# Taking a pair of heads through each pass of 256 rows in one group of four tiles, also where the pass crosses two batches

## The chip, the cores and the metric

The kernel runs on one core of a Trainium2 chip. The metric is the device time of one execution in microseconds; the changed kernel is compared with the kernel before on the same chip.

## What is computed

`q`, `k` and `v` have 8 batches, 8 heads, 576 rows and 64 columns a head. Attention keeps the 32 largest scores of each row; the result, reshaped to rows of 512, goes through a channel mix whose input is blended with the row before it.

```
scores = scale * np.matmul(q, k.transpose(0, 1, 3, 2))
kth = np.partition(scores, -top_k, axis=-1)[..., -top_k:-top_k + 1]
scores = np.where(scores >= kth, scores, -1000000000.0)
attn = np.exp(scores - np.max(scores, axis=-1, keepdims=True))
attn = attn / (np.sum(attn, axis=-1, keepdims=True) + 1e-09)
x = np.matmul(attn, v)                      # then (B, S, 512)
xk = mu_k * x + (1.0 - mu_k) * x_prev       # x_prev: the row before, 0 at a batch's start
xr = mu_r * x + (1.0 - mu_r) * x_prev
k = np.maximum(xk @ w_k, 0.0)
out = 1.0 / (1.0 + np.exp(-(xr @ w_r))) * (k * k @ w_v)
```

## The kernel before

**Tiles and slots.** A tile is 128 partitions of scores against all 576 keys. Mostly these are 128 rows of one head; two heads (a pair, `hp`, 0 to 3) and 128 rows make two tiles. A unit of four tiles is a pair of heads and 256 rows, a unit of two is 128 rows, and a unit of one tile is 64 rows of both heads. There are 288 tiles, and the program is written out by hand as a software pipeline of one slot a tile: `ORDER` lists the steps of a slot, and in slot n tile n is scored (`scores`, `keep`), tile n−1 and n−2 go through the search for the largest (`candidates`, `best`, `drop`), n−3 is counted (`count` on ACT, `below` on POOL: the tile `sg`), n−4 masked, n−5 turned (`turn_tile`), and behind the last tile of a unit (n−6) its sums are turned (`turn_inverse`) and its values weighed (`weigh`, PE), then taken out (`take_sums`, ACT) and multiplied into `xT` (`place`, POOL).

**Passes.** I call 16 slots, that is 256 of the 4608 rows for all four pairs, a pass, and number them 0 to 17. A batch ends inside passes 2, 4, 6, 11, 13 and 15. `PARTS` says how the 576 rows of each batch are cut, and a pass with an end of a batch is taken in two rounds: the rest of the old batch for all four pairs, then the start of the next for all four. In passes 2, 6, 11 and 15 the cut falls at 64 or 192 rows, so units of one tile occur.

**Loads.** Keys of a pair have one of four homes (`KEYS`); SP issues all loads and stores in the program's order, keys and queries four or five slots ahead, values (two buffers) when the unit two before has been weighed.

**Channel mix.** For each 256 finished rows a chunk starts (`chunks`, `have`, `begin`): POOL blends (`xd`, `xm`), ACT and POOL split into `xh` and `xl`, and PE multiplies in steps of three matmuls (`three`): 8 into `pz`, 32 into `ph`, and, for the chunk before, 16 into `pv`. Between `ph` and `pv` stand ACT (`r`, `hh`) and POOL (`r`, `hl`), in units of two blocks of 128; the last `pv` of a tile of rows needs the last `hl`. Two or one of these steps make a piece, and `work` deals pieces into the slots by a budget of PE time: `L.use("pe", ...)` books the steps of attention, and a piece goes in while enough is left. POOL and ACT work of the mix is dealt in the same way (`L.soft`). From slot 252 on (`END`, `HASTE`) the budget is looser. Each chunk so follows some two passes behind, and behind the last score what is left is drained, with DVE in place of POOL (`g.by`).

**Spared rows.** A chunk that starts in one batch and ends in the next first copies the rest of the old batch into `rest` (`save`), so that its buffer comes free.

Of the kernel before, what the change touches and what calls it, by code (L numbers as in the profile page):

```python
# [47 lines left out]
def topk_attention_channel_mix(ctx: ExitStack, tc: tile.TileContext, q, k, v, mu_k, mu_r, w_k, w_v, w_r, out):  # L48
# [31 lines left out]
    def open_pools(stack, g, sfx):  # L80
# [102 lines left out]
    def load_v(g, P, batch, hp):
        P.v = g.two.tile([128, 2, NKC, D], F32, name="v_in")
        P.vr = vr_hf[P.n % 2]
        h = heads(v, batch, hp)
        for j in range(2):
            nc.sync.dma_start(P.v[:, j], h[j, :MAIN].rearrange("(c p) d -> p c d", p=128))
        nc.sync.dma_start(P.vr[64:], h[:, MAIN:].rearrange("h p d -> p h d"))

    def units_of(shape):

        units, tiles = [], []
        for row, w in shape:
            U = Env()
            U.row, U.w = row, w
            units.append(U)
            for k in range(w):
                T = Env()
                T.U, T.k, T.t, T.u, T.j, T.row = U, k, len(tiles), k // 2, k % 2, row + k // 2 * 128  # L200
                T.last = k == w - 1
                tiles.append(T)
        return units, tiles
# [85 lines left out]
    def inverse(g, U):  # L289
        rs = U.rs[:, :U.w]  # L290
        nc.scalar.activation(rs, rs, AF.Copy, bias=1e-9)

    def inverse2(U):
        rs = U.rs[:, :U.w]
        nc.vector.reciprocal(rs, rs)

    def spread(g, U):
        w, d = U.w, 64 if U.w > 1 else 128
        U.rb = g.one.tile([128, w, d], F32, name="rb")
        nc.gpsimd.tensor_scalar(U.rb, U.rs[:, :w, None].to_broadcast([128, w, d]), 1.0, 1.0, op0=OP.mult, op1=OP.mult)  # L300

    def turn_inverse(g, U, L):
        rb = U.rb.rearrange("p h d -> p (h d)")
        pr = g.pt[:, :, 384:]
        n = (U.w + 1) // 2
        for u in range(n):
            nc.tensor.transpose(pr[:, u], rb[:, u * 128:(u + 1) * 128], ident)

        def out_():
            U.ri = g.two.tile([128, 256], F32, name="ri")  # L310
            if U.w > 1:
                nc.scalar.activation(U.ri[:, :n * 128].rearrange("p (u q) -> p u q", u=n), pr[:, :n], AF.Copy)
            else:
                for j in range(2):
                    h = slice(j * 64, (j + 1) * 64)
                    nc.scalar.activation(U.ri[h, :64], pr[h, 0, h], AF.Copy)
        L.at(0, "late", out_)

    def weigh(g, U, u):
        P = U.P  # L320
        if u == 0:
            U.pa = g.sums[U.w == 1]
        hs = [slice(j * 64, (j + 1) * 64) for j in range(2)]
        if U.w > 1:
            pa = U.pa[:, u]
            ms = [[U.et[u, j][:, c, :] for j in range(2)] for c in range(NKC + 1)]
        else:
            pa = U.pa
            ms = [[U.et[0, 0][:, c, h] for h in hs] for c in range(NKC + 1)]
        for c in range(NKC + 1):  # L330
            for j in range(2):
# [288 lines left out]
    def pipeline(g):  # L620
# [360 lines left out]
```

## Time and profile before

| | us |
|---|---|
| median of 3 runs (1161.68 to 1163.26) | 1162.88 |
| the profiled execution | 1162.55 |
| its span | 1160.7 |
| busy: PE, DVE, ACT, POOL | 1094.9, 1073.9, 991.4, 968.3 |

The span is the time from the first instruction to the last in the trace of one execution. Busy is the time in which an engine has an instruction under way; the ends of matmuls are modelled. PE's weight loads run beside its matmuls and have a row of their own, PEld. Each matmul of scores or of the weighing shows as two records.

### The profile page before, as it was taken

The page shows a single profiled execution, that of the slowest core. Times are in us where ns is not written, and L with a number is a line of the kernel's source. Part 1 is how long each engine was busy: PE and PEld are TensorE (multiplying, and loading weights), DVE is VectorE, ACT ScalarE, POOL GpSimd, SP SyncE. Part 2 cuts the span into 40 slices and gives each one's busy share as a digit, 9 for nine tenths or more (in the row PEclk, how much of TensorE's full clock was granted, in tenths as well). Part 3 has the DMA queues.
Part 4 walks back from the last instruction along what each step waited for, and adds up shares of the span by engine and source line. Part 5 has one row for each costly group of instructions (what it writes and reads, how often), then busy time and mean ns, then how long its engine had stood idle before and what let it go on. Part 6 is the DMA issues. An engine that isn't in the chain of part 4 may idle for free.

```text
span 1160.7 us, 32775 instructions
## 1 busy us (share of the span) xinstructions
PE 1094.9 (94%) x10625; PEld 854.2 (74%) x10625; DVE 1073.9 (93%) x6009; ACT 991.4 (85%) x2121; POOL 968.3 (83%) x1069
## 2 busy tenths in 40 slices
PE   5777999999999999999999999999999999999998
PEld 2444776768787877787878777787878777878787
DVE  6999999999999999999999999999999999989742
ACT  5889999988898899989898989998989899879631
POOL 5898997998989798989898988898989898979800
PEclk9889999999999999999999999999999999999999
DMA  7434133113331233112211132212331223111100
GB/s 193 124 111 112 30 91 92 49 45 78 77 79 45 64 74 96 49 50 69 70 49 50 29 104 68 69 45 75 80 79 45 62 73 85 44 49 40 30 10 30
DMA packets 161363, 78.77 MB, mean 68 GB/s; under 512 B 125344, under 2 KB 154016, under 8 KB 161184
## 3 DMA queue, kind: packets, MB, share of 16 engines
q1 hardware_dynamic: 161184, 76.59, 25.1%
q8 instruction: 87, 1.43, 0.5%
q14 instruction: 92, 0.75, 0.2%
HBM read 67.11 MB, written 9.44 MB: 66 GB/s over the span
## 4 chain that ended last, share of the span: by engine, by line
PE 51%; POOL 18%; DVE 16%; ACT 12%; issue 2%; DMA 1%; SPq 0%; ACTq 0%; POOLq 0%; DVEq 0%
PE ps L333 10%; PE ps L210 7%; POOL sg L260 6%; PE pt L283 4%; DVE cand L243 4%; PE ph L388 3%; PE pv L388 3%; DVE E L271 3%; PE pv L390 3%; PE ph L389 3%; PE ph L390 3%; DVE seen L843 3%; PE pv L389 3%; PE pz L388 3%; ACT sc L219 3%
## 5 line engine op out<-in xcount | busy, mean ns | idle before, releaser
L243 DVE MAX8 cand<-sc 128x8 f32<-128x82 f32 (+1 forms) x2016 | 467.2, 232 | 10.5 <-ACT sc L219 10.4
L260 POOL TENSOR_TENSOR sg<-sc,sg 128x576 f32<-128x576 f32 x288 | 411.7, 1431 | 48.7 <-ACT sg L257 48.5
L219 ACT ACTIVATE sc<-ps 128x576 f32<-128x576 f32 x288 | 188.0, 653 | 99.6 <-PE ps L210 85.8
L271 DVE SCALAR_TENSOR_TENSOR E<-sc,seen,se 128x576 f32<-128x576 f32 x288 | 232.9, 809 | 0.7 <-DVE cand L243 0.3
L257 ACT ACTIVATE sg<-sc,seen 128x576 f32<-128x576 f32 x288 | 225.7, 784 | 4.4 <-DVE seen L843 3.4
L268 ACT ACTIVATE se<-sc,seen 128x576 f32<-128x576 f32 x288 | 215.7, 749 | 10.4 <-DVE E L271 10.1
L843 DVE MAX8 seen<-sg 128x8 f32<-128x576 f32 x288 | 216.5, 752 | 4.1 <-POOL sg L260 3.7
L210 PE MATMUL ps<-K,qs 64*128 64x288 f32 x1024 | 198.7, 464 | 11.6 <-ACT sc L219 6.3
L286 ACT ACTIVATE et<-pt 128x640 f32<-128x640 f32 x288 | 204.3, 710 | 6.0 <-PE pt L283 4.0
L283 PEld LDWEIGHTS pt<-ident,E 64*128 64x128 f32 x2880 | 132.9, 139 | 75.2 <-ACT sg L257 17.5
L246 DVE MAX8 seen<-cand 128x8 f32<-128x56 f32 x864 | 177.4, 205 | 0.1
L388 PE MATMUL ph<-xh,wk 128*128 128x256 f32 x576 | 172.2, 299 | 0.0
L333 PE MATMUL ps<-et,v_in 128*64 128x128 f32 (+1 forms) x2560 | 162.0, 269 | 8.4 <-ACT sc L219 7.2
L389 PE MATMUL ph<-xl,wk 128*128 128x256 f32 x576 | 162.2, 282 | 0.0
L390 PE MATMUL ph<-xh,wk 128*128 128x256 f32 x576 | 162.0, 281 | 0.0
L333 PEld LDWEIGHTS ps<-et,v_in 128*64 128x64 f32 x2560 | 131.4, 138 | 39.6 <-ACT sc L219 13.1
L283 PE MATMUL pt<-ident,E 64*128 64x64 f32 x2880 | 140.3, 224 | 15.3 <-DVE E L271 9.0
L210 PEld LDWEIGHTS ps<-K,qs 64*128 64x128 f32 x1024 | 79.5, 189 | 74.0 <-issue 24.7
L388 PE MATMUL pv<-wv,hh 128*128 128x512 f32 x288 | 123.7, 429 | 0.0
L390 PE MATMUL pv<-wv,hl 128*128 128x512 f32 x288 | 114.3, 397 | 8.7 <-POOL hl L409 8.7
L249 DVE MATCH_REPLACE8 cand<-seen,cand 128x56 f32<-128x56 f32 x576 | 115.4, 200 | 0.0
L389 PE MATMUL pv<-wv,hh 128*128 128x512 f32 x288 | 113.5, 394 | 0.0
(103 smaller groups left out, 2234.5 us busy)
## 6 DMA issues: line engine op xcount, KB each, us to landing
v_in<-in_v SPq DMA_DIRECT2D x192, 128.0 KB, 2.6
qs<-in_q SPq DMA_DIRECT2D x96, 128.0 KB, 2.9
K<-in_k SPq DMA_DIRECT2D x64, 144.0 KB, 3.0
out<-eb SPq DMA_DIRECT2D x36, 256.0 KB, 2.5
vr_in<-in_v SPq DMA_DIRECT2D x96, 32.0 KB, 2.5
hh<-in_moe_w_v SPq DMA_DIRECT2D x6, 512.0 KB, 4.1
qs<-in_q SPq DMA_DIRECT2D x32, 96.0 KB, 2.6
hh<-in_moe_w_k SPq DMA_DIRECT2D x5, 512.0 KB, 4.2
```

The source lines that it names most:

```text
L210: nc.tensor.matmul(g.ps[:, e], lhsT=P.qs[h, T.j, x:x + 128], rhs=P.K[h, T.j], start=True, stop=True)
L219: nc.scalar.activation(T.sc.rearrange("p (e k) -> p e k", e=2), T.ps, AF.Copy)
L243: nc.vector.max(T.cand[:, 8 * i:8 * i + 8], T.sc[:, CUTS[i]:CUTS[i + 1]])
L257: nc.scalar.activation(T.side, T.sc, AF.Sign, bias=T.top[:, 23:24], scale=-1.0, accum_out=T.cnt)
L260: nc.gpsimd.tensor_mul(T.side, T.sc, T.side)
L271: nc.vector.scalar_tensor_tensor(T.e, T.sc, T.thr, g.pe, op0=OP.is_ge, op1=OP.mult, accum_out=T.rs)
L283: nc.tensor.transpose(g.pt[:, n, c * 64:(c + 1) * 64], T.e[h, k0:k0 + 128], ident[h, h])
L333: nc.tensor.matmul(pa[hs[j]], lhsT=lhsT, rhs=ms[c][j], start=(c == 0), stop=(c == NKC))
L388: nc.tensor.matmul(ps, lhsT=sh, rhs=mh, start=first, stop=False)
L389: nc.tensor.matmul(ps, lhsT=sh, rhs=ml, start=False, stop=False)
L390: nc.tensor.matmul(ps, lhsT=sl, rhs=mh, start=False, stop=last)
L843: nc.vector.max(M.top[:, 24:32], M.side)
```

## The change

The units of one, two or four tiles go. A pass is taken as four groups, one for each pair of heads, of four tiles each, also where a batch ends in it: `Part` holds the rows of one batch in a group, and a group has one part or two. Where a cut falls inside 128 rows, both tiles of these rows are made of two quarters each: 64 rows with the keys of the old batch, 64 with those of the next, and they are weighed with the values of the one and of the other in 64 columns. Everything that was done once a unit is done once a group. The planner of homes for the keys picks the home whose keys are needed last, values are loaded for each part, and the copy into `rest` is left to the moment at which a batch's buffer is needed, which does not occur.

```
-WHOLE = [(0, 4), (256, 4), (512, 1)]
-PARTS = [[(0, 4)], [(256, 4)], [(512, 1)]], [[(0, 1), (64, 2)], [(192, 4)], [(448, 2)]], \
-    [[(0, 2)], [(128, 4)], [(384, 2), (512, 1)]], [[(0, 1)], [(64, 4)], [(320, 4)]]
+BLOCK = 64
+ROWS = 4 * BLOCK
...
+        x, (Q, R) = T.u * 128, P.blocks[T.u]
+        if Q is R:
             for e, h in enumerate(hs):
-                nc.tensor.matmul(g.ps[:, e], lhsT=P.qs[h, T.j, x:x + 128], rhs=P.K[h, T.j], start=True, stop=True)
+                nc.tensor.matmul(g.ps[:, e], lhsT=P.qs[h, T.j, x:x + 128], rhs=Q.K[h, T.j], start=True, stop=True)
         else:
-            for j in range(2):
+            for i, N in enumerate((Q, R)):
                 for e, h in enumerate(hs):
-                    nc.tensor.matmul(g.ps[hs[j], e], lhsT=P.qs[h, j, x:x + 64], rhs=P.K[h, j], start=True, stop=True)
+                    nc.tensor.matmul(g.ps[hs[i], e], lhsT=P.qs[h, T.j, x + i * 64:x + (i + 1) * 64], rhs=N.K[h, T.j], start=True, stop=True)
...
+    def weigh(g, P, u):
+        Q, R = P.blocks[u]
+        for q, N in [(slice(0, 128), Q)] if Q is R else zip(hs, (Q, R)):
+            for c in range(NKC + 1):
                 for j in range(2):
...
+                    lhsT = N.v[:, j, c, :] if c < NKC else N.vr[:, j]
+                    nc.tensor.matmul(g.sums[hs[j], u, q], lhsT=lhsT, rhs=P.et[u, j][:, c, q], start=(c == 0), stop=(c == NKC))
...
+    def place(P, Q):
+        rows, cols = slice(1 + Q.row, 1 + Q.row + Q.m), slice(Q.c0, Q.c0 + Q.m)
+        nc.gpsimd.tensor_mul(Q.xT[:, P.hp, rows], P.sum[:, cols], P.ri[:, cols])
...
+                    home = max((h for h in range(KEYS) if held[h][0] < max(n - 1, 0) and ahead[h] > n), key=lambda h: (ahead[h], -held[h][0]))
+                    keys[n, b] = home, max(4 * n - (5 if n > 1 else 4), 4 * held[home][0] + 4)
...
+                vs[n, b] = len(users) % 2, max(4 * n - 2, 4 * users[-2] + 10 if len(users) > 1 else 0)
...
                     if C.pieces is None:
                         state["start"] = t0
-                        save(size)
...
             def inv():
                 if last:
-                    L.use("pe", 0.27 * W.U.w + 0.30)
+                    L.use("pe", 1.38)
...
-                    if T is U.P.tiles[-1]:
-                        state["heads"][U.P.hp] = U.P.b * S + U.row + max(64, U.w * 64)
...
+                    state["heads"][P.hp] = (P.p + 1) * ROWS
```

How this moves the instructions is seen at three places. ACT, in pass 4, where a batch ends at 128 rows: `rs` is the sum's addition of 1e-9, `ri` the copy of a unit's turned inverse, `sum` that of its weighed values. First before:

```order
L219 ACTIVATE sc<-ps 128x576
L339 ACTIVATE sum<-ps 128x128
L286 ACTIVATE et_4792<-pt 128x2x5x64
L257 ACTIVATE sg,cnt<-sc,seen 128x576
L268 ACTIVATE se<-sc,seen 128x576
L405 ACTIVATE r<-ph 128x512
L219 ACTIVATE sc<-ps 128x576
L286 ACTIVATE et_4868<-pt 128x2x5x64
L312 ACTIVATE ri<-pt 128x128
L407 ACTIVATE hh<-r 128x512
L257 ACTIVATE sg,cnt<-sc,seen 128x576
L268 ACTIVATE se<-sc,seen 128x576
```

and the same two slots of the changed kernel:

```order
L222 ACTIVATE sc<-ps 128x576
L287 ACTIVATE et_4718<-pt 128x2x5x64
L260 ACTIVATE sg,cnt<-sc,seen 128x576
L271 ACTIVATE se<-sc,seen 128x576
L386 ACTIVATE r<-ph 128x512
L222 ACTIVATE sc<-ps 128x576
L287 ACTIVATE et_4791<-pt 128x2x5x64
L308 ACTIVATE ri<-pt 128x256
L364 ACTIVATE xh<-xm 128x512 x2
L260 ACTIVATE sg,cnt<-sc,seen 128x576
L271 ACTIVATE se<-sc,seen 128x576
```

Before, each second slot has an `ri` and each second a `sum` of 128 columns; after, both come every fourth slot, with 256.

POOL, in pass 8, around the last `hl` of a chunk, which the last `pv` steps of PE need three slots behind the last `ph` (`sg` marks a slot, `rb` is the spread of the inverse sums, `xl` a half of the split of the next chunk, `xT` the product with the weighed values). Before:

```order
L260 TENSOR_TENSOR sg<-sc,sg 128x576 x2
L300 TENSOR_SCALAR rb<-rs 128x256
L384 TENSOR_TENSOR xl<-xm,xh 128x512 x2
L260 TENSOR_TENSOR sg<-sc,sg 128x576
L408 TENSOR_TENSOR r<-r 128x512
L409 TENSOR_TENSOR hl<-r,hh 128x512
L260 TENSOR_TENSOR sg<-sc,sg 128x576
```

and of the change:

```order
L263 TENSOR_TENSOR sg<-sc,sg 128x576
L365 TENSOR_TENSOR xl<-xm,xh 128x512 x2
L263 TENSOR_TENSOR sg<-sc,sg 128x576
L593 MEMSET xT 128x4
L325 TENSOR_TENSOR xT<-sum,ri 128x256
L389 TENSOR_TENSOR r<-r 128x512
L390 TENSOR_TENSOR hl<-r,hh 128x512
L263 TENSOR_TENSOR sg<-sc,sg 128x576
```

The product into `xT` now stands in the slot of the last `hl`, ahead of it, and the pair of `xl` directly in the slot before (the `MEMSET` comes once a batch).

DVE, behind the last tile, where it has taken over POOL's part (`eb` is the output of a tile of rows, taken from the `pv` just done). Before:

```order
L408 TENSOR_TENSOR r<-r 128x512
L409 TENSOR_TENSOR hl<-r,hh 128x512
L384 TENSOR_TENSOR xl<-xm,xh 128x512 x2
L363 TENSOR_SCALAR xm<-xd_19890,nmu 128x256 x2
L368 TENSOR_TENSOR xm<-xm,xT 128x512
L363 TENSOR_SCALAR xm<-xd_20072,nmu 128x256 x2
L368 TENSOR_TENSOR xm<-xm,xT 128x512
L429 SCALAR_TENSOR_TENSOR eb<-eb,pv 128x512
L384 TENSOR_TENSOR xl<-xm,xh 128x512 x2
L429 SCALAR_TENSOR_TENSOR eb<-eb,pv 128x512
```

and of the change:

```order
L410 SCALAR_TENSOR_TENSOR eb<-eb,pv 128x512 x2
L365 TENSOR_TENSOR xl<-xm,xh 128x512 x2
L344 TENSOR_SCALAR xm<-xd_19702,nmu 128x256 x2
L349 TENSOR_TENSOR xm<-xm,xT 128x512
L344 TENSOR_SCALAR xm<-xd_19419,nmu 128x256 x2
L349 TENSOR_TENSOR xm<-xm,xT 128x512
L365 TENSOR_TENSOR xl<-xm,xh 128x512 x2
```

The two `eb` of the last chunk but one have moved ahead of the last chunk's first `xl`; on PE all its `pv` now stand ahead of the last `pz`, where eight steps stood between the last `pz` and the last `ph`.

## Rows read from the trace of the kernel before

**Rows 1.** The page, part 1: busy us, share of the span, instructions.

```profile
PE 1094.9 (94%) x10625; PEld 854.2 (74%) x10625; DVE 1073.9 (93%) x6009; ACT 991.4 (85%) x2121; POOL 968.3 (83%) x1069
```

**Rows 2.** Windows: passes 2–3, 4–7, 8–10, 11–14, 15, 16, 17, the end.

```profile
core 0: us, PE busy (x) PEld busy (x) DVE busy (x) ACT busy (x) POOL busy (x), PEclk, DMA share, GB/s
143.60:260.40 116.80, 110.03 (x1182) 84.90 (x1178) 114.31 (x666) 106.44 (x241) 103.06 (x120) 0.99 0.27 69
260.40:493.80 233.40, 230.71 (x2352) 182.44 (x2346) 227.15 (x1320) 212.05 (x467) 209.44 (x238) 1.00 0.27 70
493.80:666.70 172.90, 172.01 (x1688) 139.16 (x1684) 170.15 (x982) 155.94 (x319) 154.21 (x153) 1.00 0.20 53
666.70:900.20 233.50, 229.29 (x2346) 182.50 (x2342) 227.53 (x1322) 212.60 (x468) 207.68 (x233) 1.00 0.27 70
900.20:961.50 61.30, 59.68 (x635) 45.61 (x633) 57.50 (x333) 54.12 (x123) 52.98 (x62) 1.00 0.28 73
961.50:1025.80 64.30, 61.75 (x613) 49.65 (x613) 59.30 (x340) 54.77 (x124) 58.88 (x72) 0.97 0.24 63
1025.80:1084.60 58.80, 57.11 (x555) 46.21 (x551) 53.33 (x307) 49.36 (x100) 48.64 (x49) 1.00 0.16 40
1084.60:1160.70 76.10, 68.76 (x494) 59.42 (x490) 32.49 (x86) 26.25 (x49) 15.41 (x17) 0.98 0.05 19
```

**Rows 3.** Windows of pass 9, of the tiles ph, pv, pz in turn.

```profile
551.50:609.10 57.60, 13.43 (x96) 12.01 (x96) 2.38 (x4) 1.00 0.23 60
551.50:609.10 57.60, 12.87 (x48) 8.48 (x48) 1.36 (x2) 1.00 0.23 60
551.50:609.10 57.60, 6.55 (x24) 4.28 (x24) 1.19 (x2) 1.00 0.23 60
```

**Rows 4.** Groups by line: busy us, mean ns, idle before them.

```profile
L307 PE MATMUL pt<-ident,rb 128*128 128x128 f32 x160 | 42.3, 313 | 3.6 <-POOL rb L300 3.0
L300 POOL TENSOR_SCALAR rb<-rs 128x128 f32<-128x128 f32 (+1 forms) x112 | 39.3, 350 | 9.4 <-DVE cand L243 7.9 <-PE pt L307 0.9 <-DVE least L878 0.3
L295 DVE RECIPROCAL rs<-rs 128x4 f32<-128x4 f32 (+2 forms) x112 | 17.5, 156 | 10.1 <-ACT rs L291 9.8
L345 POOL TENSOR_TENSOR xT<-sum,ri 128x256 f32<-128x256 f32 x48 | 35.8, 745 | 31.5 <-ACT sum L339 31.3
```

**Rows 5.** Groups by line and form: weighing in 128 and in 64 columns.

```profile
L333 PE MATMUL ps<-et,v_in 128*64 128x128 f32 x2048 | 140.1, 280 | 7.3 <-ACT sc L219 7.2
L333 PE MATMUL ps<-et,v_in 128*64 128x64 f32 x512 | 21.9, 228 | 1.1 <-ACT sum L339 0.6 <-ACT sum L341 0.3
```

**Rows 6.** Timeline of pass 5: start us, us, engine line, idle before and releaser.

```profile
357.70 0.76 PE L210 MATMUL ps<-K,qs 64*128 64x288 f32 x4
...
357.80 2.54 POOL L384 TENSOR_TENSOR xl<-xm,xh 128x512 fp32r<-128x512 f32 x2
...
360.28 0.66 ACT L407 ACTIVATE hh<-r 128x512 fp32r<-128x512 f32 x1
360.29 1.44 POOL L260 TENSOR_TENSOR sg<-sc,sg 128x576 f32<-128x576 f32 x1
...
360.97 0.76 PE L210 MATMUL ps<-K,qs 64*128 64x288 f32 x4
...
361.67 1.06 POOL L408 TENSOR_TENSOR r<-r 128x512 f32<-128x512 f32 x1
...
362.81 1.27 POOL L409 TENSOR_TENSOR hl<-r,hh 128x512 fp32r<-128x512 f32 x1
...
364.13 0.51 PE L390 MATMUL pv<-wv,hl 128*128 128x512 f32 x1 [1.43 <-POOL hl L409]
```

**Rows 7.** Timeline of pass 8: scores around a slot with a weighing.

```profile
539.26 0.76 PE L210 MATMUL ps<-K,qs 64*128 64x288 f32 x4
...
544.02 0.76 PE L210 MATMUL ps<-K,qs 64*128 64x288 f32 x4
```

**Rows 8.** Timeline of the end, behind the last pz.

```profile
1127.32 0.60 ACT L421 ACTIVATE eb<-pz 128x512 f32<-128x512 f32 x1 [2.21 <-PE pz L390]
...
1128.47 1.29 DVE L384 TENSOR_TENSOR xl<-xm,xh 128x512 fp32r<-128x512 f32 x2 [4.78 <-ACT xh L383]
```

More of the change, by code (lines that the diff above doesn't have):

```diff
@@ L183, in load_v, with __init__ @@
[L183 to L186, printed above, removed]
-        for j in range(2):
[L188 to L203, printed above, removed]
+    class Part:
+        def __init__(self, b, row, c0, m, batch):
+            self.b, self.row, self.c0, self.m, self.batch = b, row, c0, m, batch
@@ new lines, in load_v, with open_group @@
+    def load_v(g, Q, hp, which):
+        Q.v = g.two.tile([128, 2, NKC, D], F32, name="v_in")
+        Q.vr = vr_hf[which]
+        h = heads(v, Q.batch, hp)
+        for j in range(2):
+            nc.sync.dma_start(Q.v[:, j], h[j, :MAIN].rearrange("(c p) d -> p c d", p=128))
+        nc.sync.dma_start(Q.vr[64:], h[:, MAIN:].rearrange("h p d -> p h d"))
+    def open_group(P):
+        of = [Q for Q in P.parts for _ in range(Q.m // BLOCK)]
+        P.blocks = [of[2 * u:2 * u + 2] for u in range(2)]
+        P.tiles, P.et = [], {}
+        for t in range(4):
+            T = Env()
+            T.P, T.t, T.u, T.j = P, t, t // 2, t % 2
+            T.last = t == 3
+            P.tiles.append(T)
@@ L287, in turn_tile, with inverse @@
         L.at(*EVAC, out_)
[L289 to L303, printed above, removed]
+    def inverse(g, P):
+        nc.scalar.activation(P.rs, P.rs, AF.Copy, bias=1e-9)
@@ L309, in out_ @@
         def out_():
[L310 to L313, printed above, removed]
-                for j in range(2):
[L315 to L331, printed above, removed]
-                lhsT = P.v[:, j, c, :] if c < NKC else P.vr[:, j]
-                nc.tensor.matmul(pa[hs[j]], lhsT=lhsT, rhs=ms[c][j], start=(c == 0), stop=(c == NKC))
@@ L641, in pipeline @@
-        xT, tiles, state = {}, {}, {"heads": [0] * HP, "wait": 0, "start": 0, "held": []}
+        groups = []
+        for p in range(B * S // ROWS):
+            parts, o = [], p * ROWS
+            while o < (p + 1) * ROWS:
+                b, row = divmod(o, S)
+                m = min(S - row, (p + 1) * ROWS - o)
+                parts.append((b, row, o - p * ROWS, m))
+                o += m
+            groups += [(p, hp, parts) for hp in (range(HP) if p % 2 == 0 else reversed(range(HP)))]
@@ new lines, in pipeline @@
+        keys, held, loads_ = {}, [(-1, None)] * KEYS, 0
+        for n, (p, hp, parts) in enumerate(groups):
+            for b, *_ in parts:
+                home = next((h for h, (_, of) in enumerate(held) if of == (b, hp)), None)
+                if home is None:
+                    ahead = [next((m for m in range(n, len(groups)) if of and groups[m][1] == of[1] and any(x[0] == of[0] for x in groups[m][2])), len(groups)) for _, of in held]
+                    home = max((h for h in range(KEYS) if held[h][0] < max(n - 1, 0) and ahead[h] > n), key=lambda h: (ahead[h], -held[h][0]))
+                    keys[n, b] = home, max(4 * n - (5 if n > 1 else 4), 4 * held[home][0] + 4)
+                held[home] = n, (b, hp)
@@ L643, in save @@
+        vs, users = {}, []
+        for n, (p, hp, parts) in enumerate(groups):
+            for b, *_ in parts:
+                vs[n, b] = len(users) % 2, max(4 * n - 2, 4 * users[-2] + 10 if len(users) > 1 else 0)
+                users.append(n)
+        xT, tiles, state = {}, {}, {"heads": [0] * HP, "wait": 0, "start": 0, "held": [], "K": {}}
         def save(size=CH):
@@ L656, in chunks @@
                 C = Env()
-                C.n, C.rows, C.pieces = size, out_rows[t0:t0 + size], None
+                C.n, C.rows, C.pieces, C.first, C.begun = size, out_rows[t0:t0 + size], None, t0 // S, 0
+                state["chunk"] = C
                 def have(i, C=C, t0=t0, size=size):
```

249 lines of the change are left out of this document (118 added, 131 removed).

## The prediction

> **What bounds the kernel now.** I read the share of each engine first [rows 1]: TensorE (PE) is busy for 1094.9 of 1160.7 us, VectorE (DVE) for 1073.9, ScalarE (ACT) and GpSimd (POOL) for 991.4 and 968.3. An average hides the stages, so next I cut the run into passes: a pass is 256 rows of the flattened output, 16 slots, and I took the start of every sixteenth copy of scores out of PSUM as its edge [rows 2]. Passes 8 to 10, where no batch ends, take 172.9 us, 57.6 each. In them PE is idle for 0.9 us, DVE for 2.75, ACT and POOL for 17 and more. So PE is the bound, DVE follows closely, and what ACT and POOL are spared is hidden behind both. In the passes where a batch ends, and just behind them, PE idles more: 2.7 us in 4 to 7, 4.2 in 11 to 14, 6.8 in 2 and 3 (there DVE is busy for 114.31 of 116.8), 2.6 in pass 16, at a granted clock of 0.97. PE's work hardly changes here; where it waits, and in which pass it does its share of the channel mix, does.
>
> **The channel mix** fills PE in steps of three matmuls ("threes"), 56 for a chunk of 256 rows: 32 into `ph`, 16 into `pv`, 8 into `pz`. A three costs 0.42, 0.80 and 0.82 us of PE [rows 3] (13.43, 12.87 and 6.55 us over their numbers; these are bounds from above, since matmuls overlap).
>
> **What the change removes.** Per run 112 units become 72 groups.
> - PE: 16 of 160 turnings of the inverse sums, 42.3/160 = 0.26 us each [rows 4]: 4.2 us at most. They are inside the windows from which I sum, so I do not book them twice.
> - DVE: 40 of 112 reciprocals at 0.156 us, 6.2 us, and 6 of 24 reductions into `least`. DVE has 0.9 us to spare in a regular pass, so I book a gain only where DVE is the bound, in passes 2 and 3.
> - ACT: 40 additions of 1e-9, and two or three copies for each unit that goes. POOL: 40 of 112 spreads, 16 products, the six copies into `rest`. Both engines already idle for 17 us and more in three passes; this costs and brings nothing as long as PE or DVE stays ahead. Were that cover gone, the spreads alone would bring 40·0.35 = 14 us.
> - The tiles of two batches: four score matmuls on quarters of the array, and twenty weighings of 64 columns in place of ten of 128, are as many as before (32 tiles, 16 groups). With 32 records of `v_in` the half of a group costs 32·21.9/512 = 1.37 us in 64 columns, with 16 it costs 16·140.1/2048 = 1.09 in 128 [rows 5]; four pairs of heads make 1.1 us a mixed pass, before as after.
>
> **What it adds.** 24 more loads of keys (56 for 32), since in a mixed pass two pairs of heads must be fetched again. Each is issued at least four slots, some 14 us, ahead of its use, and the DMA engines are busy for 0.20 to 0.28 of the time [rows 2]. SP issues in order, so queries, values and results stand behind a load that waits for its home; the home comes free with the last score four slots before. The values of a mixed group wait for the weighing of the group ahead and have three slots, 10.8 us. I take 0 for both; if a load came a slot late in each mixed pass it would be 6·3.6 = 22 us, which nothing in these leads supports.
>
> **What it moves.** The rhythm. Now units end after one, two or four tiles, so that in a mixed pass and the one behind it a weighing stands in up to every slot, and the mix is dealt by what is left. After the change PE's order in passes 4 to 14 is the same in every pass: 56 threes, a weighing in each fourth slot. Before, those passes held 55, 57, 54, 54, 56, 56, 56, 50, 56, 55 and 57. Ten threes more are thus done there, and three more in pass 15.
>
> What could spoil this rhythm is one place: the last values wait for `hl`. Now in pass 5 [rows 6]: POOL takes the pair `xl` at 357.80, then `sg`, `r`, and `hl` until 364.08, and PE, which wanted it 1.43 us earlier, waits. In passes 8 to 10 ACT makes `hh` a slot earlier and PE's idle time leaves no room for such a wait. POOL's order after the change is that of pass 5, in every pass, with one step more: the product into `xT`, 0.745 us [rows 4], comes between `sg` and `r`. In return `xl` falls into the slot with the weighing, which is longer: 544.02 − 539.26 = 4.76 us [rows 7] against 360.97 − 357.70 = 3.27 [rows 6], so it can begin up to 1.5 us earlier against the next score. Counted from that score: `xl` from −1.4 to 1.15, `sg` to 2.6, product to 3.3, `r` to 4.4, `hl` to 5.65; PE wants it at 362.70 − 357.70 = 5.0. I take a wait of **0.65 us** a pass. The bounds are 0 (it begins another 0.65 earlier) and 1.43 + 0.745 = 2.2 (as late as in pass 5, with the product added).
>
> **The sum**, against the execution in the profile, 1162.55 us (1.85 beside the span; the median of the runs, 1162.88, is 0.03% above):
> - Passes 4 to 14: 11·57.6 + 2·1.1 + 11·0.65 = 643.0 against 233.4 + 172.9 + 233.5 = 639.8: **+3.2**.
> - Pass 15: 57.6 + 1.1 + 0.65 + 3·0.80 = 61.75 against 61.3: **+0.45**.
> - Passes 2 and 3: eight reciprocals fewer in pass 2 where DVE is the bound, 8·0.156: **−1.3** (bounds: 0, and −3 if half of PE's idle time goes).
> - Pass 16: 60 threes become 54, six fewer into `pz`, 6·0.82 = 4.9; DVE holds the pass above 57, and one empty slot appears. 64.3 becomes 59.8: **−4.5** (bounds −2 and −6).
> - Pass 17: five `pv` fewer, three `pz` more: −1.5; **−1** is taken, as DVE must keep up.
> - The end: 109 threes instead of 117 stand behind the last score, 3·0.80 + 5·0.82 = 6.5 us fewer. But before, 24 value matmuls stood between the last `pz` and the last `ph` and covered the way over `xh` and `xl` (ACT 1127.32 to DVE 1129.76 [rows 8]); after, nothing does, and PE waits for about 1.7; the first `xl` stands behind two `eb`, the second of which needs all values: about 1 more, and 0.7 for `low`. **−3** (bounds −6 and 0).
>
> Together −6.15: **1156.4 us**.
>
> **Rivals.**
> 1. *It becomes slower: the wait for `hl` in every pass.* Each 0.1 us of it costs 1.2 us over passes 4 to 15, so the gain is gone at a wait of 0.65 + 6.15/12 = 1.16 us, and the kernel slower by over 0.2% from 1.35 on. At pass 5's 1.43 it takes 1165.8, at 2.2 us 1175. For it: this wait stands in the profile [rows 6], in the very order that now comes in each pass. Against it: the longer slot [rows 7].
> 2. *Nothing measurable.* PE's work is the same but for 4.2 us, and passes 16, 17 and the end only give back what passes 2 to 15 took on, 16 threes. Then about 1162. For it: PE 99.5% busy where it is undisturbed [rows 2]. Against: PE's idle 20 us in passes 2 to 17.
> 3. *DVE is what counts.* Its 7 us of dropped reciprocals and reductions come off, the rest moves nothing: 1155.2. For it: the 98.4% of passes 8 to 10; against it PE's idle time there, a third of DVE's. The Trainium skill, "Perfetto Trace Analysis", section "Identifying the Most-Contended Engine", states that for TensorE the busy share of matmuls is no good measure and the share of weight loads should be read, for VectorE occupancy. By it (74% for weight loads, 93% for DVE [rows 1]) DVE is the engine to relieve, and the time would be this rival's; the rows of the regular passes speak for PE.
>
> **How the numbers follow.** Forecast 0.45 (own range 1153 to 1160), rival 1 0.22, rival 2 0.20, rival 3 0.13. Two tenths of a percent, 2.3 us, is about what can be told from no change here. Forecast and rival 3 are faster: 0.58; rival 2: 0.20; rival 1: 0.22. The range reaches from 1150, where the wait is 0.1 us and the rest as taken, to 1167, where it is 1.5.
>
> **What would show it.** In the profile after: equal passes of 58.2 us from 4 on; a wait of PE `pv` for POOL `hl` of 0.3 to 1.0 us in each; pass 16 below 61; in the end two waits of PE, around the last `pz`. Wrong would be: waits for `hl` above 1.35 us; PE waiting for K, queries or values; regular passes at 57.6 or below, which would show that the wait was absorbed.

## The result, and the profile after

The changed kernel takes 1168.94 us (median of 5 runs, 1167.89 to 1169.6) where the kernel before takes 1162.58 beside it: a ratio of 1.0056, 95% interval 1.0041 to 1.007. It is slower by 0.56%. 1156.4 was predicted, in a range of 1150 to 1167. Among the runs below, one execution of the kernel with the product last and the values later took 2548.77 us and is left out of its ratio.

The page of the changed kernel, part 1, answers to [rows 1], and the groups by line to [rows 4]:

```profile
PE 1094.0 (94%) x10609; PEld 850.5 (73%) x10609; DVE 1073.7 (92%) x5959; ACT 971.2 (83%) x1969; POOL 958.9 (82%) x1011
```

```profile
L304 PE MATMUL pt<-ident,rb 128*128 128x128 f32 x144 | 31.9, 304 | 6.0 <-POOL rb L298 5.2
...
L298 POOL TENSOR_SCALAR rb<-rs 128x256 f32<-128x256 f32 x72 | 29.6, 411 | 1.2 <-DVE cand L246 1.2
...
L294 DVE RECIPROCAL rs<-rs 128x4 f32<-128x4 f32 x72 | 11.8, 164 | 13.3 <-ACT rs L291 13.2
```

The change does what it says: 72 spreads for 112, 144 turnings for 160, 40 reciprocals fewer. No engine is busier than before (VectorE just as busy, 1073.7 us for 1073.9, although 5.7 us of reciprocals went), but the span is 1167.8 us for 1160.7. So the loss is idle time, and the windows say where. They are the same passes as [rows 2], with their edges found in the same way (2–3, 4–7, 8–10, 11–14, 15, 16, 17, the end):

```profile
core 0: us, PE busy (x) PEld busy (x) DVE busy (x) ACT busy (x) POOL busy (x), PEclk, DMA share, GB/s
146.70:264.80 118.10, 111.19 (x1188) 86.45 (x1185) 114.26 (x654) 102.89 (x212) 100.94 (x108) 0.97 0.31 76
264.80:500.50 235.70, 230.41 (x2353) 183.25 (x2352) 227.69 (x1308) 207.25 (x425) 207.65 (x223) 1.00 0.30 76
500.50:676.20 175.70, 172.10 (x1685) 137.78 (x1685) 170.51 (x981) 155.49 (x321) 153.91 (x152) 1.00 0.23 59
676.20:912.20 236.00, 230.35 (x2349) 183.00 (x2349) 227.83 (x1308) 207.32 (x427) 207.70 (x223) 1.00 0.31 79
912.20:973.10 60.90, 59.93 (x641) 46.28 (x639) 57.27 (x329) 52.07 (x107) 51.99 (x54) 1.00 0.30 77
973.10:1034.10 61.00, 56.63 (x602) 45.43 (x598) 57.40 (x327) 50.29 (x103) 46.76 (x51) 1.00 0.27 71
1034.10:1093.60 59.50, 57.19 (x547) 46.69 (x543) 55.16 (x312) 50.17 (x103) 54.59 (x57) 0.97 0.14 35
1093.60:1167.80 74.20, 65.06 (x469) 55.94 (x464) 29.61 (x82) 24.88 (x47) 16.79 (x17) 0.96 0.06 20
```

Passes 8 to 10 show it best, since no batch ends there and the same groups of four stood there before: PE is busy for 172.1 us in both kernels, but the passes take 175.7 us for 172.9, and its idle time goes from 0.9 to 3.6. The list of waits names the cause on its face (us in total, times, longest):

```profile
PE pv L371 <- POOL hl L390: 15.2, 14, 1.4
```

The wait for the last `hl` now stands in every pass from 3 to 16. In passes 4 to 14 it is 0.79 to 1.34 us long and 12.46 in all, 1.13 on average. In pass 8 it looks so (timeline of ACT, POOL and PE apart: start us, us):

```profile
533.58 1.15 ACT L364 ACTIVATE xh<-xm 128x512 fp32r<-128x512 f32 x2
```

```profile
533.38 1.44 POOL L263 TENSOR_TENSOR sg<-sc,sg 128x576 f32<-128x576 f32 x1
534.77 2.53 POOL L365 TENSOR_TENSOR xl<-xm,xh 128x512 fp32r<-128x512 f32 x2
537.25 1.44 POOL L263 TENSOR_TENSOR sg<-sc,sg 128x576 f32<-128x576 f32 x1
538.64 0.73 POOL L325 TENSOR_TENSOR xT<-sum,ri 128x256 f32<-128x256 f32 x1
539.33 1.04 POOL L389 TENSOR_TENSOR r<-r 128x512 f32<-128x512 f32 x1
540.45 1.27 POOL L390 TENSOR_TENSOR hl<-r,hh 128x512 fp32r<-128x512 f32 x1
...
547.49 0.40 POOL L298 TENSOR_SCALAR rb<-rs 128x256 f32<-128x256 f32 x1
```

```profile
540.23 0.39 PE L370 MATMUL pv<-wv,hh 128*128 128x512 f32 x1
541.78 0.50 PE L371 MATMUL pv<-wv,hl 128*128 128x512 f32 x1 [1.15 <-POOL hl L390]
```

The order on POOL is the one predicted: `xl`, `sg`, the product into `xT`, `r`, `hl` (the excerpt of this order shown with the change, which has the `MEMSET`, is of pass 9). From the start of `xl` to the end of `hl` it takes 6.95 us; PE is free for it after 5.86 (540.63).

### The profile page after: what moved, and what is told of

Its sections match the earlier page's. It is cut to its first block, busy times and chain, and to the rows that moved or that the text cites. A ratio compares the mean times of both kernels' runs of the same rounds, so it can differ in the third digit from the quotient of the medians.

```text
span 1167.8 us, 32519 instructions
## 1 busy us (share of the span) xinstructions
PE 1094.0 (94%) x10609; PEld 850.5 (73%) x10609; DVE 1073.7 (92%) x5959; ACT 971.2 (83%) x1969; POOL 958.9 (82%) x1011
## 3 DMA queue, kind: packets, MB, share of 16 engines
q8 instruction: 87, 1.43, 0.5%
## 4 chain that ended last, share of the span: by engine, by line
PE 39%; POOL 32%; DVE 19%; ACT 5%; issue 3%; SPq 1%; DMA 1%; ACTq 0%; POOLq 0%
POOL sg L263 10%; PE ps L317 7%; PE ps L213 5%; POOL hl L390 5%; DVE cand L246 4%; POOL r L389 4%; DVE E L274 4%; PE pv L369 3%; POOL xl L365 3%; PE pv L371 3%; DVE seen L826 3%; PE pt L284 3%; PE pv L370 3%; PE ph L369 2%; PE pz L369 2%
## 5 line engine op out<-in xcount | busy, mean ns | idle before, releaser
L317 PE MATMUL ps<-et,v_in 128*64 128x128 f32 (+1 forms) x2560 | 158.9, 268 | 4.8 <-ACT sc L222 4.7
L369 PE MATMUL pv<-wv,hh 128*128 128x512 f32 x288 | 124.6, 433 | 0.0
L369 PEld LDWEIGHTS ph<-xh,wk 128*128 128x128 f32 x576 | 108.9, 189 | 7.7 <-ACT xh L364 1.6
```

The lines of the kernel that those rows point to most:

```text
L317: nc.tensor.matmul(g.sums[hs[j], u, q], lhsT=lhsT, rhs=P.et[u, j][:, c, q], start=(c == 0), stop=(c == NKC))
L369: nc.tensor.matmul(ps, lhsT=sh, rhs=mh, start=first, stop=False)
```

## The experiments

Where a theory has a letter in the expectations: A, the wait for `hl` is paid in full in every pass, and the start costs 3 us by a changed order of loads; B, what differs at the start is chance; C, the wait is no cost of its own, something else would take its place; D, the added loads of keys cost. From the runs on the place of the channel mix on, P says that this place against the groups costs, O that only the order in POOL's queue does, and D there stands for the groups themselves. All times below are medians beside the kernel before, and "passes 4–14" is their length in the profile, cut as above (639.8 us before, 647.4 after the change).

| kernel | us | ratio (95%) | passes 4–14 |
|---|---|---|---|
| changed, values later | 1165.97 | 1.0028 (1.0014–1.0041) | 647.1 |
| before, values earlier | 1163.38 | 1.0007 (0.9998–1.0016) | 641.0 |
| changed, product behind `hl` | 1167.96 | 1.0046 (1.0033–1.006) | 647.6 |
| changed, both of these | 1167.02 | 1.0038 (1.0024–1.0052) | 647.6 |
| changed, product twice | 1191.45 | 1.0247 (1.023–1.0264) | 665.2 |
| changed, 6 homes for keys | 1167.96 | 1.0049 (1.0036–1.0063) | 646.9 |
| changed, product last in slot | 1163.68 | 1.0015 (1.0006–1.0024) | 640.5 |
| changed, `hl` first | 1167.41 | 1.0039 (1.0026–1.0052) | 647.3 |
| changed, product last, values later | 1164.42 | 1.0015 (1.0006–1.0024) | 641.9 |
| before, product last in slot | 1167.72 | 1.0038 (1.0025–1.0051) | 640.5 |
| changed, mix held by 7 steps | 1149.64 | 0.989 (0.9875–0.9905) | 633.9 |
| the same, values later | 1149.61 | 0.9891 (0.9876–0.9906) | 633.9 |
| changed, mix held by 8 steps | 1159.8 | 0.9978 (0.9966–0.999) | 641.1 |
| changed, mix held by 3 steps | 1166.83 | 1.0043 (1.003–1.0057) | 648.6 |
| changed, two shares on ACT | 1169.53 | 1.0052 (1.0037–1.0067) | 649.2 |
| changed, all shares on ACT | 1185.81 | 1.0196 (1.0181–1.021) | 657.0 |

**The start.** In the two profiles pass 2 begins at 146.7 us for 143.6. On TensorE, ScalarE, VectorE and GpSimd the first two passes have the same order as before; on SP the values of the second group now stand ahead of the first weights. The issues of SP in the changed kernel and with the later load:

```profile
9.11 1.14 SPq L193 DMA_DIRECT2D v_in<-in_v  x2
...
10.95 0.59 SPq L148 DMA_DIRECT2D hh<-in_moe_w_r  x1
```

```profile
9.11 0.59 SPq L148 DMA_DIRECT2D hh<-in_moe_w_r  x1
...
17.53 0.44 SPq L193 DMA_DIRECT2D v_in<-in_v  x1
```

```diff
 # changed kernel
-vs[n, b] = len(users) % 2, max(4 * n - 2, ... if len(users) > 1 else 0)
+vs[n, b] = len(users) % 2, max(4 * n - 2, ... if len(users) > 1 else 6)
 # kernel before
-if n == starts[N.n - 1] + 6:
+if n == (2 if N.n == 1 else starts[N.n - 1] + 6):
```

> The changed kernel with one number changed: the values of the second group are loaded at slot 6, as before, and not at slot 2, where they stand ahead of the first weights in SP's order. Theory A (a part of the loss comes from the start, where the first weight load is issued 1.83 us later, at 10.95 us for 9.12): pass 2 begins some 3 us earlier, near 143.6 us, and the time falls from 1168.9 to about 1166. Theory B (the start differs by chance from run to run, and the loss is all in the passes): pass 2 still begins at about 146.7 us, and the time stays within 1 us of 1168.9.

> The kernel before with this one part of the change alone: the values of the second visit are loaded at slot 2. Theory A: pass 2 begins at about 146.7 us and the time rises from 1162.6 to about 1165.7. Theory B: no difference beyond 1 us.

The later load took 3.0 us off the changed kernel's median, the earlier one put 1.0 on the kernel before. But three other pairs that differ only by the same edit give −0.9 (with the product behind `hl`), 0.0 (with the mix held by seven) and +0.7 (with the product last in its slot): a mean of −0.8 over the four. In the profiles, passes 0 and 1 of eight changed kernels with the early load and nearly the same order at the start take 137.3 to 139.2 us, of the four with the late one 137.6 to 137.8; the kernel with the product last, which orders the start otherwise, took 140.5 with the early load. So about 1 us of the 3.1 between the first two profiles is this load. The rest is within what executions spread by, as far as one profile of each kernel shows: B is nearer than A, and a single pair of profiles had misled me.

**The order in POOL's queue.** First the product into `xT` of every fourth group was put behind `hl`, alone and with the later load.

```diff
-place(P, Q)
+if P.n % HP:
+    place(P, Q)
+else:
+    state.setdefault("late", []).append((P, Q))
...
 def judge():
+    for late in state.pop("late", []):
+        place(*late)
```

> The changed kernel, in which for the first group of each pass the product into xT is issued at the end of its slot, behind the last hl of a chunk, and no longer in front of it; nothing else moves. Theory A (PE is the bound, and each us of its wait for the last hl is a us of the pass): the wait falls from 1.12 us by up to 0.75 to some 0.4, passes 4 to 14 fall from 58.9 to about 58.2 us, and the time falls by 7 to 9 us, to about 1161. Theory C (the passes are bound by DVE and the wait is absorbed, or another wait takes its place): the wait is shorter, but the passes keep 58.7 us or more and the time stays above 1167.

> Both edits, the late load of the second values and the product behind the last hl. Theory A: the gains add up, 3 and 7 to 9 us, to about 1158, some 4 to 5 us below the kernel before at 1162.6. Theories B and C: 1167 to 1169, and slower than the kernel before by 0.4% or more.

A expected 7 to 9 us less; 1.0 came. The rows of POOL and PE in pass 8 of this kernel:

```profile
533.51 2.51 POOL L365 TENSOR_TENSOR xl<-xm,xh 128x512 fp32r<-128x512 f32 x2
...
538.50 1.29 POOL L390 TENSOR_TENSOR hl<-r,hh 128x512 fp32r<-128x512 f32 x1
...
546.23 0.40 POOL L298 TENSOR_SCALAR rb<-rs 128x256 f32<-128x256 f32 x1
```

```profile
539.84 0.50 PE L371 MATMUL pv<-wv,hl 128*128 128x512 f32 x1 [0.49 <-POOL hl L390]
...
546.68 0.44 PE L304 MATMUL pt<-ident,rb 128*128 128x128 f32 x2 [0.67 <-POOL rb L298]
```

The wait for `hl` fell by 0.66 us, as a product of 0.73 should make it, and a wait of 0.67 for the spread inverses `rb` took its place. From the start of `xl` to the end of `rb` POOL works without a pause: 546.63 − 533.51 = 13.12 us here, 547.89 − 534.77 = 13.12 in the changed kernel. What the product leaves ahead of `hl` it adds behind it. C was right in its second half (another wait takes its place), not in its first (VectorE as the bound).

Then `hl` with its rounding and square was dealt ahead of all other waiting work.

```diff
-h = L.soft("act", 0.5, ..., out_, rank=1)
+h = L.soft("act", 0.5, ..., out_, rank=-1)
 # and q and X.done likewise
```

> The changed kernel with the rounding hh, the square r and the rest hl dealt ahead of other waiting work of ScalarE and GpSimd (a rank of -1 for 1). The mix keeps its early place (slots 2 to 7), and the amount of work of GpSimd stays; only hl comes before the shares and before xl. Theory O (order): the wait for hl goes, passes 4 to 14 take 57.6 to 57.8 us, 1156 to 1160 in all. Theory P (position): GpSimd's backlog stays and comes out elsewhere, at sg or rb or xl; passes 4 to 14 stay within 58.3 to 59.2, 1164 to 1170. Theory D: as P, but with VectorE busy to within 0.5 us of each pass.

The wait for `hl` is gone from passes 4 to 14; they take 647.3 us all the same. (The mix also stands one step earlier here.) In the list of waits now stands

```profile
PE pt L304 <- POOL rb L298: 18.9, 25, 1.5
```

with 0.65 to 1.53 us in each of them. O falls: the wait that the profile names can be removed, and nothing is won, since the same queue is late at its next customer.

The product made twice asks for the price of the wait in the other direction.

```diff
 def place(P, Q):
...
     nc.gpsimd.tensor_mul(Q.xT[:, P.hp, rows], P.sum[:, cols], P.ri[:, cols])
+    if P.n >= 0 and P.n % HP == 0:
+        spare = g.one.tile([128, 256], F32, name="spare")
+        nc.gpsimd.tensor_mul(spare[:, cols], P.sum[:, cols], P.ri[:, cols])
```

> The changed kernel with the suspected cost doubled: for the first group of each pass POOL does the product twice, the second time into a spare tile that nobody reads, ahead of the last hl; 18 products of some 0.75 us. Theory A: the wait of PE for the last hl grows from 1.12 to about 1.85 us in each pass and the time rises by 8 to 10 us, to about 1178. Theory C: the time rises by less than 2 us.

Windows of passes 8 and 9, and PE's wait in pass 9:

```profile
505.00:564.30 59.30, 57.34 (x561) 45.96 (x561) 56.81 (x327) 51.79 (x108) 51.92 (x52) 1.00 0.22 58
564.30:625.10 60.80, 58.93 (x561) 47.01 (x561) 57.04 (x327) 51.96 (x109) 52.05 (x53) 0.97 0.21 57
```

```profile
606.20 0.50 PE L374 MATMUL pv<-wv,hl 128*128 128x512 f32 x1 [1.87 <-POOL hl L393]
```

The wait grows by 0.7, and pass 8 by 0.6 (59.3 for 58.7): added to the chain, POOL's time is paid in full, so VectorE does not absorb it, and C is wrong there. The rest of the 22.5 us is told in the last section.

**The loads of keys.** With two more homes the keys are loaded 32 times, as before the change, for 56 in the changed kernel.

```diff
-KEYS = 4
+KEYS = 6
```

> The changed kernel with six homes for the keys in place of four, so that fewer keys are fetched again (the loads of keys fall from 112 to 88 or fewer). Theory A (loads are hidden): the time stays within 1 us of 1168.9. Theory D (the added loads cost, by SP's order or by traffic, some of the loss): the time falls by 2 us or more.

1.0 us less than the changed kernel, with intervals that overlap, and passes 4 to 14 within 0.5 us of its own. The added loads are hidden, as predicted.

**The place of the channel mix.** What differs between the regular passes of the two kernels is where the mix stands against the groups. In passes 8 to 10 TensorE did, slot by slot, 3 1 3 3 4 2 6 6 6 2 6 4 3 1 3 3 threes before, and 3 1 5 6 6 2 6 6 4 1 3 3 3 1 3 3 after the change (the slots with 1 or 2 and a weighing are the second, sixth, tenth and fourteenth). A step of the mix is two `ph` threes or one other three, and by steps the mix begins its `ph` seven earlier. A first edit moves it by opening a chunk a slot later:

```diff
-ORDER = """... mask place mix wpe weigh dve pool judge weights""".split()
+ORDER = """... mask mix wpe weigh dve pool place judge weights""".split()
```

> The changed kernel with the product into xT put at the end of its slot, behind the other work of GpSimd there. A chunk is then open a slot later, and the whole channel mix comes later against the groups: from pass 8 on the steps of six threes stand in slots 6 to 10, as in passes 8 to 10 of the kernel before, in place of slots 2 to 7. Theory P (position): with the mix early, GpSimd has to make the shares of the next chunk between the first and the last square, has no idle time from there to the last values, and PE pays; with the mix late the shares fall behind the squares. Passes 8 to 14 take 57.6 to 57.9 us, without a wait for hl above 0.4; pass 16 and the end take back 3 to 5 us, since more threes are left for them; 1159 to 1163 us in all. Theory D (the groups themselves, VectorE): passes 8 to 14 stay at 58.5 to 59.2, 1166 to 1171. Theory O (only the order of hl in the queue of GpSimd): as P for this kernel.

> The product into xT at the end of its slot, and the values of the second group loaded at slot 6, behind the first weights. If the two effects add up: P gives 1156 to 1160 us, 2 to 3 us less than with the product alone at the end; D gives 1163 to 1168.

> The kernel before with the product into xT at the end of its slot: its mix, too, comes about a slot later (in passes 8 to 10 the sixes stand in slots 7 to 12 in place of 6 to 11). Theory P: passes 8 to 10 keep 57.6 us, because GpSimd has spare time there already; passes 4, 5, 13 and 14, whose mix stands early, lose their waits for hl of 1 to 1.4 us; 1157 to 1162 in all. Theory D: the same as before, 1161 to 1164.

In the changed kernel passes 8 to 14 went from 58.4–59.2 to 58.1–58.3 us, half of what P expected: the wait for `hl` is gone, another stands in its place (below), and the total is still 0.15% over the kernel before. The later load brought nothing beside it. The same edit in the kernel before shortens pass 5, which loses its wait of 1.43 us [rows 6], from 58.5 to 57.0, and leaves 9 and 10 at 57.5 and 57.4; but waits for `hl` of 0.88, 1.02 and 0.70 us stand in passes 4, 13 and 14, pass 17 is 5.3 us longer, where PE now waits 2.77 us for `hl`, and the whole nearly 6. P expected these waits to go and the whole to be shorter, and was wrong on both.

So the mix was moved by itself: TensorE does no mix in two slots of pass 3, once, and keeps the place that this gives.

```diff
+HOLD = (50, 51)
...
-work(MOST)
+if n not in HOLD:
+    work(MOST)
```

Slots 50 and 51 hold it by seven steps in effect, 52, 54 and 55 by eight, 50 and 53 by three (they skip four, and one is made up in the same pass).

> The changed kernel whose channel mix is held for two slots once, in pass 3. From pass 4 on every pass then has, slot by slot, the threes that passes 8 to 10 of the kernel before have (3 1 3 3 4 2 6 6 6 2 6 4 3 1 3 3), seven steps of the mix later than the change left it; nothing else is moved. Theory P (position of the mix): passes 5, 8, 9, 10, 13 and 14 take 57.5 to 57.8 us, the mixed ones and those behind them up to 58.6, without a wait for hl above 0.4; pass 16 has 61 threes for 54 (3 to 5 us longer), the end 105 for 109 (2 to 3 shorter), pass 3 45 for 52 (0 to 3 shorter); 1155 to 1162 in all. Theory D (the groups themselves cost): passes 58.2 or more, 1165 to 1170.

> The same hold, and the values of the second group loaded at slot 6, behind the first weights. If the start and the position of the mix are two separate costs, 1 to 3 us less than with the hold alone; by P 1153 to 1160, below both kernels; by D 1162 to 1168.

> The mix is held by one step more than in the kernel with the hold of seven (steps 3 1 3 3 3 2 6 6 6 2 6 5 3 1 3 3, which are those of passes 8 to 14 with the product at the end of its slot, but with the product in its old place). P: if one step decides, since the last rounding hh then falls into the slot of both xh on ScalarE, regular passes take 58.1 to 58.3 us with a wait of the weighing for the copy of scores of 0.6 to 0.7, as with the product at the end; if it was the moved product that cost there, 57.6. D: 58.5 or more in both kernels.

> The mix is held by one slot and one step in pass 3, so that it stands half-way (3 1 3 5 6 2 6 6 6 2 3 3 3 1 3 3), as pass 4 of the kernel before has it. P: between the early and the late place, regular passes of 57.8 to 58.9 us; a wait for hl of 0.4 to 1.3 stays, since the sixes still end ahead of the last shares. D: 58.5 or more. In all 1158 to 1168.

Held by seven steps the changed kernel takes 1149.64 us, 1.1% less than the kernel before. Its windows of passes 4–7, 8–10, 11–14 and 16, and ACT, POOL and PE in pass 9:

```profile
261.00:492.00 231.00, 229.63 (x2358) 184.35 (x2354) 226.65 (x1309) 207.85 (x425) 207.87 (x223) 1.00 0.30 78
492.00:664.30 172.30, 171.46 (x1688) 138.62 (x1686) 169.98 (x982) 156.07 (x318) 154.16 (x153) 1.00 0.22 58
664.30:894.90 230.60, 229.54 (x2358) 184.22 (x2353) 226.65 (x1309) 208.03 (x424) 207.69 (x221) 1.00 0.31 82
...
954.80:1018.50 63.70, 60.99 (x621) 49.24 (x617) 57.78 (x328) 52.77 (x107) 53.92 (x60) 1.00 0.24 64
```

```profile
593.43 1.15 ACT L365 ACTIVATE xh<-xm 128x512 fp32r<-128x512 f32 x2
...
594.15 2.53 POOL L366 TENSOR_TENSOR xl<-xm,xh 128x512 fp32r<-128x512 f32 x2 [0.71 <-ACT xh L365]
596.63 1.43 POOL L264 TENSOR_TENSOR sg<-sc,sg 128x576 f32<-128x576 f32 x1
597.99 1.06 POOL L390 TENSOR_TENSOR r<-r 128x512 f32<-128x512 f32 x1
599.13 1.28 POOL L391 TENSOR_TENSOR hl<-r,hh 128x512 fp32r<-128x512 f32 x1
...
597.12 1.09 PE L318 MATMUL ps<-et,v_in 128*64 128x128 f32 x16 [0.27 <-ACT sc L223]
...
601.01 0.40 PE L372 MATMUL pv<-wv,hl 128*128 128x512 f32 x1
```

The time is below what P expected, since besides the 13.5 us of passes 4 to 14 the hold saves 3.2 in passes 2 and 3, 1.0 in pass 15 and 2.9 at the end, and gives back 2.7 in pass 16. PE idles 1.4 us in passes 4 to 7, 5.3 without the hold. Regular passes take 57.4 to 57.6 (6 and 11, with tiles of two batches, 58.5 and 58.1), and no wait for `hl` is left in passes 4 to 14. The chain is short, 600.41 − 594.15 = 6.26 us, since the product comes behind `hl`; and PE wants it late, at 601.17 − 594.15 = 7.02, since a weighing lies between. With the mix early the weighing stands for the most part ahead of `xl`, and the product in the chain.

Eight steps give about 58.2 us a pass, and PE waits 0.46 to 0.68 us ahead of the weighing (pass 8):

```profile
534.68 0.60 ACT L387 ACTIVATE r<-ph 128x512 f32<-128x512 f32 x1
...
538.41 0.59 ACT L387 ACTIVATE r<-ph 128x512 f32<-128x512 f32 x1
...
540.00 1.16 ACT L365 ACTIVATE xh<-xm 128x512 fp32r<-128x512 f32 x2
541.04 0.65 ACT L389 ACTIVATE hh<-r 128x512 fp32r<-128x512 f32 x1
...
542.99 0.66 ACT L223 ACTIVATE sc<-ps 128x576 f32<-128x576 f32 x1
```

From 534.68 on ACT works without a pause, and makes the last two `r`, their `hh` and both `xh` ahead of this copy of scores, which the weighing needs. With seven steps the first of these `r` is made a slot earlier, ahead of 0.73 us in which ACT idles, and the wait is 0.27. So one step decides, but not as P had put it: the last `hh` stands behind both `xh` with seven steps too. The kernel with the product last in its slot has its mix in the same place and shows the same passes (58.1 to 58.3), so the moved product is not to blame there. Three steps bring nothing: 58.5 to 60.5, a wait for `hl` of 0.87 to 1.56 in every pass, both longer than P expected.

**Whose queue it is.** P as I had put it blamed POOL's work from the first square `r` on. The last two kernels take scalings of the shares off POOL, with TensorE's order unchanged up to pass 15.

```diff
-nc.gpsimd.tensor_scalar(X.xm[:, h, :n], g.change[i][:, h, :n], nmu[...], 1.0, ...)
+nc.scalar.activation(X.xm[:, h, :n], g.change[i][:, h, :n], AF.Copy, scale=nmu[...])
```

> The changed kernel, its mix in its early place, TensorE's order as it is; only the two scalings of the shares of the second two pairs (0.94 us of GpSimd a pass, between the first and the last square) are made on ScalarE, which idles for 7 us a pass. If GpSimd's queue from the first square on carries the cost (theory P), the wait for hl shrinks by about as much, from 1.13 to 0.1 to 0.5 us, and no other wait takes its place: regular passes 57.6 to 58.1, 1155 to 1163 in all. If the place of the mix costs on TensorE or ScalarE whatever GpSimd does, passes stay at 58.4 or more, 1165 to 1171.

> All eight scalings of the shares (3.8 us of GpSimd a pass) are made on ScalarE, up to the last passes. P: no wait for hl is left, regular passes 57.4 to 57.8, 1153 to 1161; the bound of that is ScalarE, whose added 3 to 4 us could make the copies of scores late (a wait of the weighing for them of up to 0.7, as with the hold of eight): then 58.0 to 58.3, 1160 to 1165. Position on TensorE alone: 58.4 or more.

Neither helps. In the first, the edit reached the stretch ahead of `hl` in every second pass only, since the pairs of heads change their order; in these the wait is hardly shorter, 1.05 us for 1.19 in pass 9. With all shares on ACT (pass 9):

```profile
598.86 2.53 POOL L370 TENSOR_TENSOR xl<-xm,xh 128x512 fp32r<-128x512 f32 x2 [0.33 <-ACT xh L369]
```

POOL now idles ahead of `xl`, which begins when ACT has `xh`, and PE waits 1.08 us for `hl` as before, and 0.79 more for a copy of scores that ACT brings late. So POOL's work ahead of `xl` is not the cause. What counts begins at `xl`. Counted from there in pass 9:

| kernel | until `hl` is there | until PE wants it | PE waits |
|---|---|---|---|
| changed | 6.99 | 5.86 | 1.19 |
| product behind `hl` | 6.34 | 5.88 | 0.51 |
| product twice | 7.65 | 5.83 | 1.87 |
| all shares on ACT | 7.00 | 5.98 | 1.08 |
| held by 3 | 6.25 | 4.97 | 1.34 |
| held by 7 | 6.26 | 7.02 | – |
| held by 8 | 6.25 | 6.53 | – |

Each wait is the difference of the two, plus 0.05 or 0.06. This account was made after the runs, and no run was made to test it; its two terms are measured apart, though: the product is worth 0.65 (second row), the weighing between 1.1 (7.02 less 5.9).

That these waits are paid in full can be read from the eighteen kernels side by side. Less the waits of PE that are longer than 0.15 us, pass 9 takes 57.1 to 57.4 us in seventeen of them, whatever the order, and 58.9 in the one with the product twice, whose clock fell there. The kernels differ in which waits are left: 0.27 us in pass 9 with the hold of seven, 0.30 in the kernel before, 1.19 in the changed one, 2.24 with all shares on ACT.

## Why the prediction was wrong

The sign was wrong. The miss is 13.3 us (7.1 of span measured, −6.15 predicted); passes 4 to 14, the start and passes 2 and 3 make up 10.1 of it.

| stretch | predicted | measured |
|---|---|---|
| start (passes 0, 1) | 0 | +3.1 |
| passes 2, 3 | −1.3 | +1.3 |
| passes 4–14 | +3.2 | +7.6 |
| pass 15 | +0.45 | −0.4 |
| pass 16 | −4.5 | −3.3 |
| pass 17 | −1 | +0.7 |
| end | −3 | −1.9 |

- **The wait for `hl`**, "I take a wait of 0.65 us a pass", is the step that failed most: it measured 1.13, 5.3 us more over eleven passes, and carries the 4.4 by which passes 4 to 14 were mis-sized. The steps of the chain were right to a few tenths, and so was the time at which PE wants it (5.0 us after the score). The start was not: `xl` was to begin 1.4 us ahead of the score and began 0.87 ahead (534.77 against 535.64, pass 8), since neither ACT's `xh` (until 534.73) nor POOL's `sg` (until 534.82) was done earlier. In pass 5 before, too, `xl` began only as ACT's `xh` ended (356.70 + 1.16, row below); I did not ask what would hold it, and let the longer slot give the chain its whole length.
- **The reading behind it** went further wrong: I booked the weighing as a help because it falls beside `xl`. In passes 8 to 10 before, the chain was as short and PE as late as with the hold of seven (6.27 and 7.04 us in pass 8, rows below); the weighing helps where it lies between `xl` and the values. I had the two orders of TensorE side by side and read from them only that the new one was regular, and took 57.6 us from passes whose mix stands elsewhere. That the place costs is shown by the hold of seven: 633.9 us for 647.4 with nothing else moved. Nor would a shorter wait for `hl` alone have saved the forecast: with `hl` dealt first it is gone, and passes 4 to 14 still take 647.3 us, since `rb`, from the same queue, is late in its place.
- **The start** was missing from the sum. Of its 3.1 us about 1 is the load of values ahead of the weights, which I should have found: the change moves these loads ahead in SP's order. No run ties the rest to the change.
- **Passes 2 and 3** gained nothing from eight reciprocals. PE's granted clock there is 0.97 for 0.99, at its lower level of 1.2 GHz for 6.8 us from 189.5 on, among waits of 0.75 to 0.83 us, where before it was so for 3.4; what part is the change's I could not settle.
- **Pass 16** had the right sign, and three quarters of the predicted size came; PE idles 4.4 us there, where I had one empty slot of a mean 3.6. **The end** shows the predicted waits around the last `pz` (0.92 and 1.20, and 0.55 for `low`); 1.9 for 3 us is within the bounds. **Pass 17** was off by 1.7, with the clock at 0.97.
- **Rival 1** came true, at a mean wait below its threshold of 1.16, because the start and passes 2 and 3 added to it. In passes 4 to 14 none of the signs set for a wrong prediction came (the longest wait is 1.34 us, the sign was 1.35). **Rival 3** did not: the reciprocals went and the time rose. By the rule of the Trainium skill, "Perfetto Trace Analysis", section "Identifying the Most-Contended Engine", VectorE was the engine to relieve. It is busy for 1073.7 us after the change, 1073.9 before and 1068.0 with the hold of seven, while the time of the changed kernel moves by 19 us with that hold; no run here shows VectorE as the bound of a regular pass, though none relieves VectorE alone.
- **Right** were the loads of keys as hidden, the unchanged work of TensorE, the equal passes and the order on POOL. What the groups themselves are worth is seen with the mix in its old place: passes 4 to 14 take 633.9 us for 639.8, as the irregular passes of before are gone. Whether the kernel before would gain from another place of its mix is open: the one other place tried, with the product last, made it longer.

The rows of the kernel before for the first two points, ACT in pass 5, then POOL and PE in pass 8:

```profile
356.70 1.16 ACT L383 ACTIVATE xh<-xm 128x512 fp32r<-128x512 f32 x2
...
538.72 2.54 POOL L384 TENSOR_TENSOR xl<-xm,xh 128x512 fp32r<-128x512 f32 x2 [0.82 <-ACT xh L383]
...
541.69 1.09 PE L333 MATMUL ps<-et,v_in 128*64 128x128 f32 x16 [0.29 <-ACT sc L219]
...
543.72 1.27 POOL L409 TENSOR_TENSOR hl<-r,hh 128x512 fp32r<-128x512 f32 x1
...
545.36 0.40 PE L389 MATMUL pv<-wv,hh 128*128 128x512 f32 x1
```

## What to carry to other kernels

Where a change re-deals interleaved work, take the length of a stretch only from passes in which the two kinds of work already stand against each other as they will after it; a regular order can be the wrong one, and moving the whole filler by a few steps can be worth more than the change (here 19 us for a two-line hold). When a wait of the bounding engine is removed, ask whom the same queue serves next: compare the queue's unbroken stretch with the time that the engine gives it, not the one wait. And compare starts over several executions before a difference in one pair of profiles becomes a theory.

## What the runs showed of the hardware

A wait on TensorE can cost more than its length. With the product made twice, PE waits 1.62 to 1.87 us for `hl` in passes 5 to 11. Behind the wait in pass 9 the granted clock is at its lower level of 1.2 GHz for 3.4 us (from 607.0 on, mean 0.64 in the window below), and that pass takes 60.8 us; pass 8, with a wait of 1.85 and the clock at 1.00, takes 59.3. Seven of passes 7 to 15 show such a drop. In the changed kernel, whose waits are 0.8 to 1.3 us, none of passes 4 to 15 does. It is not the wait's length alone: behind 2.21 us in pass 4 the kernel with the product last kept its clock, and the one with the later load as well lost it; and behind 1.43 us in pass 5 the kernel before kept it (58.5 us), while the kernel before with the values earlier lost it from 366.1 on (60.0 us).

```profile
606.20:611.00 4.80, 4.80 (x23) 3.32 (x24) 3.22 (x15) 0.82 (x3) 4.72 (x7) 0.64 0.15 55
```
